# adaLN block with grouped-KV attention and a bilinear GLU: the q projections of later blocks as single whole-row products, a lead in smaller steps, and gate and up weights split by columns

## The chip, the cores and the metric

The kernel runs on one core of one Trainium2 chip. The metric is the device time of one execution in microseconds (us); for the kernel before, three executions were timed and the median counts. The engines are named as in the profile: PE does the matrix products (PEld is its weight load), DVE the reductions and elementwise work, ACT the activations, POOL (GpSimd) elementwise work in SBUF, SP issues DMAs. PE writes to PSUM, which has eight banks of 128 x 512 f32.

## The reference

One layer on x of 2048 x 512. A vector c gives six rows of modulation; the layer is attention and then a gated product, each behind a layer norm:

```python
mod = (_silu(c) @ w_mod).reshape(c.shape[0], 6, 1, -1)
h = _layernorm(x) * (1 + ca) + sa
q = (h @ wq)            # 32 heads of 16
k = h @ wk; v = h @ wv  # one head of 16, shared by all 32
p = _softmax(q @ k.T * 16 ** -0.5)
x = x + ga * ((p @ v) @ wo)
h = _layernorm(x) * (1 + cb) + sb
x = x + gb * (((h @ w_gate) * (h @ w_up)) @ w_down)   # width 1792
```

## The kernel before

**Numbers in halves.** f32 products take PE four passes, so the large ones are done on f16 pairs: a matrix is scaled, cut into a high and a low half, and a product is three terms (`TERMS`, line 413). `in_halves` (L374) makes the halves: ACT casts the high one, POOL scales the f32 tile in place and subtracts.

**Blocks, units, steps.** The 2048 queries are four blocks of 512 (`BT`); a block has eight units of four heads; a unit has 32 steps. In a step the main loop (L1104) issues two maximum products with their row maxima on DVE (`max_mm`, L516: the maximum of each row of scores, needed by the exponential), two score products with an exp on ACT each (`qk_exp`, L554), and at every odd step the product of the exps with v (`pv`, L563, four 32-column products in f32). The maxima run `LEAD` = 40 steps ahead of the rest, so they start in a *lead*: 40 steps with maxima alone, beside which the layer norm, k, v and q of the four blocks are prepared (`first`, L402, a table from step to work; `ln_tr` transposes, `k_mm` projects k, `h_halves` makes the f16 halves of the normed input, `v_mm` projects v in one go at step `V_STEP`). Before the lead stands a start, about 29 us, which loads, makes the first modulation and projects block 0's k and the first heads' q.

**q.** `q_proj` (L484) makes 128 columns of q for one block as a `Group` of twelve products. Two groups at a time run as a `duo` (L450): each product is cut into its upper and lower 64 rows, so that two 64-row products of the two groups run side by side; this holds two banks, misc and spare. Between its calls a duo yields, and `burst` (L1038) issues some of its pairs in a step. A group's evacuation is two ACT passes (L489, L490), one POOL subtraction and a DMA to DRAM, from where `load_q` (L503) later brings a unit's rows back. In the lead, `lead_fill` (L1068) bursts six pairs a step from step 18 on; what is left is queued for the main loop with a due step of 40 (`QDUE`). There `fill_gap` (L1013) is called at every even step, behind the second maximum product, and `pace` sets the rate by the due steps. The same queue later carries each block's output projection, second layer norm (`solo` items) and FFN groups.

**Banks.** Scores have two banks (tag sc) and, when no duo holds it, the bank spare as a third (`ps_sc`, L65); maxima have three, pv one, misc one.

**Side work.** A list of small steps (`late_weights`, L782) is issued from the main loop by `side_step` (L1054), one item at a time, each with a gap in steps to the next; an item with a PE product is only taken at odd steps, behind `pv`. In order: for each of the four late matrices (wo, wg, wu, wd) its slices are loaded and their squares added up on POOL (`square`), then the column sums are formed (`sums`, L829: four f32 products on 32 columns each, and a row maximum); the second modulation product (`m0`, four parts of four products, then `m1`, `m2`, `m3`); the scales; and then the split of wo, wg and wu into halves (`split`, L898: three POOL passes a slice, and one more for wo and wd, which are multiplied by the modulation rows gab and gbb). wg and wu are split in slices of 128 rows x 448 columns, all of wg first and then all of wu. wd follows in a list of its own.

**What the buffers share.** `kwb` holds the f32 tiles of the normed input (`hfs`, ten of them in turn) and, behind them, the sums of squares (`ssq`); wg and wu take the places of the two parts of w_mod.

Of the kernel before, what the change touches and what calls it, by code (L numbers as in the profile page):

```python
# [33 lines left out]
FILL0 = 18  # L34
QPRE = 20
QPRE0 = 26
# [4 lines left out]
NHF = 10  # L41
V_STEP = 34
DUE = 12
QDUE = 40
# [5 lines left out]
def adaln_mqa_glu_kernel(ctx: ExitStack, tc: tile.TileContext, x_in, wq_in, wk_in, wv_in, wo_in,  # L50
# [145 lines left out]
    ssq = kwb[:, 2 * NHF * BT:2 * NHF * BT + 2 * F].bitcast(F32)  # L196
# [7 lines left out]
    sck = consts.tile([128, 4], F32, name="sck")  # L204

    def ln_stats(i):
        if i % 2 == 0:
            stats[i // 2] = (work.tile([128, 4, 2], F32, name="st"), work.tile([128, 4], F32, name="ry0"),
                             work.tile([128, 4], F32, name="nb0"))
# [7 lines left out]
    def ln_norm(b):  # L217
        st, y, nb = stats[b]
        for i in range(2):
            xt = xts[2 * b + i]  # L220
            nc.vector.tensor_scalar(xt[:, 0, :], xt[:, 0, :], st[:, 2 * i, 0:1], y[:, 2 * i:2 * i + 1],
                                    op0=OP.subtract, op1=OP.mult)
            nc.scalar.activation(xt[:, 1, :], xt[:, 1, :], AF.Identity, bias=nb[:, 2 + i:3 + i],
                                 scale=y[:, 2 * i + 1:2 * i + 2])

    def ln_tr(b, ks=range(KC)):
        for k in ks:
            p = ps_sc()
            for t in range(4):
                nc.tensor.transpose(p[:, t * 128:(t + 1) * 128],  # L230
                                    xts[2 * b + t // 2][:, t % 2, k * 128:(k + 1) * 128], ident)
            nc.scalar.activation(hf(b, k), p, AF.Identity,
                                 bias=modT[0][:, k, 0:1], scale=modT[0][:, k, 32:33])
# [17 lines left out]
    def k_evac(b):  # L251
        cs = slice(b * BT, (b + 1) * BT)
        split_rows(kst[:, cs], pks[b], sck[:, 0:1], sck[:, 2:3], rows[:, 6:7])

    def ln_rstd(b):
        st, y, nb = stats[b]
        rstd_into(y, st[:, :, 1], 4)
        nc.gpsimd.tensor_tensor(nb[:, 0:2], st[:, 1:4:2, 0], y[:, 1:4:2], op=OP.mult)
        nc.gpsimd.tensor_scalar(nb[:, 2:4], nb[:, 0:2], -1.0, 0.0, op0=OP.mult, op1=OP.add)
# [68 lines left out]

    q0_mm(0)
# [6 lines left out]
    nc.gpsimd.tensor_scalar(inv[:, 0:1], kb[:, 4:5], 22.64 * 1.001 * 2.0 ** -15, 2.0 ** -45, op0=OP.mult, op1=OP.max)  # L336
# [31 lines left out]
    def wq_scales():  # L368
        nc.vector.reciprocal(fwd, inv)
# [4 lines left out]
    def in_halves(hi, lo, t, scale):  # L374

        nc.scalar.activation(hi, t, AF.Copy, scale=scale)
        nc.gpsimd.tensor_scalar(t, t, scale, 0.0, op0=OP.mult, op1=OP.add)
        nc.gpsimd.tensor_tensor(lo, t, hi, op=OP.subtract)  # L378

    def h_halves(b, ks=range(KC)):  # L380
        cs = slice(b * BT, (b + 1) * BT)
        for k in ks:
            in_halves(h16[:, 0, k, cs], h16[:, 1, k, cs], hf(b, k), fwd[:, 0:1])

    def wq_halves(ks):
        for k in ks:
            in_halves(wq[:, 0, k, :], wq[:, 1, k, :], wqst[k], fwd[:, 1:2])
# [7 lines left out]
    def last_rows():  # L395
# [6 lines left out]
    first = {0: lambda: (q0_mm(1, KA), wq_squares()), 1: lambda: (q0_mm(1, KB), wq_sum()),  # L402
             2: lambda: (q0_evac(1), ln_tr(1, KA), wq_scales()),
             3: lambda: (ln_tr(1, KB), ln_stats(6), h_halves(0, KA)), 4: lambda: k_mm(1, KA),
             5: lambda: (k_mm(1, KB), ln_stats(7), ln_rstd(3), h_halves(0, KB)),
             6: lambda: (k_evac(1), ln_norm(2)), 7: lambda: (ln_tr(2, KA), wq_halves(KA)),
             8: lambda: (ln_tr(2, KB), ln_norm(3), wq_halves(KB)), 9: lambda: k_mm(2, KA),
             10: lambda: (k_mm(2, KB), h_halves(1, KA)), 11: lambda: (k_evac(2), h_halves(1, KB)),
             12: lambda: ln_tr(3, KA), 13: lambda: ln_tr(3, KB), 14: lambda: (k_mm(3, KA), h_halves(2, KA)),
             15: lambda: (k_mm(3, KB), h_halves(2, KB)), 16: lambda: k_evac(3),  # L410
             17: lambda: (last_rows(), ev_scales()), 25: lambda: h_halves(3, KA), 27: lambda: (h_halves(3, KB), wv_halves())}
# [4 lines left out]
    def v_mm():  # L416
        p = vt["p"] = ps_pv()
        for k in range(KC):
            for i, (wl, hl) in enumerate(TERMS):
# [795 lines left out]
```

## Time and profile before

| | |
|---|---|
| median of three executions | 1780.48 us (1777.08 to 1782.25) |
| the profiled execution, its own time | 1779.66 us |
| its span in the profile | 1777.9 us |
| busy: PE, DVE, ACT, POOL | 1692.5, 1414.0, 1231.9, 509.8 us |
| first exp of unit 0 | at 105.07 us |
| mean granted clock of TensorE | 0.993 |

The page gives busy times and shares, a chain of waits that ended last, and groups of instructions by line. A group's row is: line, engine, operation, output and inputs, shapes and count, then its busy time and the mean length of one in ns, then the idle time of the engine before them and what ended it. A row of the timeline is: start and length in us, engine, line, operation, names, shapes and count (several that follow closely are merged), and in brackets the idle time before and its releaser. A row of the windows is: the stretch and its length, for each engine its busy time and number of instructions, then the granted clock, the share of the DMA engines and GB/s. The ends of matrix products are modelled and overlap, so distances between their starts tell more than their lengths.

### The profile page before, as it was taken

The numbers are of one execution on the slowest core, as the hardware profiler recorded it, in microseconds if no ns is written. First come the engines' busy times: TensorE is split into PE (matmuls) and PEld (weight loads), VectorE is DVE, ScalarE is ACT, GpSimd is POOL, SyncE is SP. The second block draws the span as 40 slices with busy tenths as digits, with TensorE's granted clock in tenths as the row PEclk, the third lists the DMA queues.
The fourth block names the chain that finished last, engine by engine and source line by source line (L and its number), as shares of the span: only waits on it lengthen the run. The fifth ranks groups of instructions, "written<-read, shape, count | busy, mean of one in ns | idle before, by whom it ended". The sixth has DMA issues, their size and how long they took to land.

```text
span 1777.9 us, 32413 instructions
## 1 busy us (share of the span) xinstructions
PE 1692.5 (95%) x12727; PEld 558.3 (31%) x12727; DVE 1414.0 (80%) x2348; ACT 1231.9 (69%) x2301; POOL 509.8 (29%) x706
## 2 busy tenths in 40 slices
PE   6899999989989999999999999999999999999999
PEld 2432222222222333333323333333323333324444
DVE  7777999989987888888898888888898899920310
ACT  4567888878876777777777777777787777774210
POOL 5833453618555941110022111010022011100330
PEclk9899999999999999999999999999999999999999
DMA  5222221212221200000100000000100000001000
GB/s 194 88 77 78 64 81 50 68 45 66 78 63 38 74 20 13 9 16 20 40 21 16 9 5 20 3 14 21 39 21 16 9 16 9 11 4 41 19 0 24
DMA packets 49797, 66.60 MB, mean 37 GB/s; under 512 B 16166, under 2 KB 30314, under 8 KB 49644
## 3 DMA queue, kind: packets, MB, share of 16 engines
q1 hardware_dynamic: 48060, 64.33, 11.6%
q8 instruction: 100, 1.64, 0.4%
q14 instruction: 53, 0.43, 0.1%
q10 hardware_dynamic: 1584, 0.20, 0.1%
HBM read 51.12 MB, written 8.92 MB: 34 GB/s over the span
## 4 chain that ended last, share of the span: by engine, by line
PE 80%; ACT 9%; DVE 5%; POOL 3%; DMA 1%; issue 1%; SPq 0%; POOLq 0%; ACTq 0%
PE pv L568 26%; PE misc L448 19%; PE mx L521 13%; PE sc L559 12%; PE misc L479 7%; ACT P L561 6%; DVE mpart L523 4%; ACT ev L574 1%; DMA wmA<-in_w_mod_dram 1%; POOL h L378 1%; POOL wu L918 0%; PE mxt L535 0%; DVE x L650 0%; ACT qf L490 0%; ACT q L489 0%
## 5 line engine op out<-in xcount | busy, mean ns | idle before, releaser
L523 DVE TENSOR_REDUCE mpart<-mx 128x1 f32<-128x512 f32 x2048 | 1298.1, 683 | 154.6 <-PE sc L559 122.9
L561 ACT ACTIVATE P<-sc 128x512 f32<-128x512 f32 x2048 | 1096.8, 597 | 326.0 <-PE sc L559 322.5
L559 PE MATMUL sc<-sst,kst 50*128 50x512 f16 x2048 | 631.1, 380 | 40.9 <-ACT P L561 35.7
L521 PE MATMUL mx<-kst,sst 48*128 48x512 f16 x2048 | 648.4, 382 | 19.3 <-DVE mpart L523 15.6
L568 PE MATMUL pv<-P,vst 128*32 128x512 f32 x4096 | 547.8, 607 | 0.0
L521 PEld LDWEIGHTS <-sst 48*128 48x128 f16 x2048 | 161.2, 94 | 586.4 <-issue 520.0
L448 PE MATMUL misc<-h2T,wu 64*128 64x512 f16 x1008 | 254.9, 376 | 2.9 <-POOL wu L917 2.1
L448 PE MATMUL misc<-h2T,wg 64*128 64x512 f16 x1008 | 254.7, 376 | 0.0
L742 POOL TENSOR_SCALAR glu<-gf 128x512 f16<-128x512 f32 x56 | 34.7, 621 | 543.5 <-DVE gf L741 543.5
L559 PEld LDWEIGHTS <-kst 50*128 50x128 f16 x2048 | 138.1, 94 | 100.7 <-issue 59.2
L568 PEld LDWEIGHTS pv<-P,vst 128*32 128x32 f32 x4096 | 80.9, 108 | 167.1 <-issue 163.9
L448 PEld LDWEIGHTS <-wu 64*128 64x128 f16 x1008 | 94.9, 94 | 63.2 <-POOL wu L917 2.6
L448 PEld LDWEIGHTS <-wg 64*128 64x128 f16 x1008 | 94.5, 94 | 52.9 <-issue 2.2
L741 DVE TENSOR_TENSOR gf<-misc,g 128x512 f32<-128x512 f32 x56 | 38.3, 683 | 89.6 <-PE misc L479 62.9
L448 PE MATMUL misc<-wd,glu 64*128 64x512 f16 x840 | 105.7, 375 | 0.0
L601 POOL TENSOR_TENSOR oc<-oc,rr 128x512 f32<-128x512 f32 x15 | 19.1, 1274 | 267.2 <-DMA rr<-ri 194.5
L735 ACT ACTIVATE g<-misc 128x512 f32<-128x512 f32 x56 | 33.5, 598 | 69.1 <-PE misc L479 63.4
L743 POOL TENSOR_TENSOR glu<-gf,glu 128x512 f16<-128x512 f32 x56 | 64.8, 1157 | 4.7
L448 PEld LDWEIGHTS <-glu 64*128 64x128 f16 x840 | 43.7, 94 | 45.6 <-issue 1.7
L825 POOL TENSOR_TENSOR wsl<-wsl 128x448 f32<-128x448 f32 (+1 forms) x40 | 39.1, 977 | 57.0 <-DMA wsl<-in_B_w_up_dram 31.1
L448 PE MATMUL misc<-h,wq 64*128 64x512 f16 x384 | 53.0, 391 | 2.4 <-ACT qf L490 2.4
L479 PE MATMUL misc<-wd,glu 128*128 128x512 f16 x252 | 55.1, 379 | 0.0
(218 smaller groups left out, 913.9 us busy)
## 6 DMA issues: line engine op xcount, KB each, us to landing
wsl<-in_B_w_gate_dram SPq DMA_DIRECT2D x32, 224.0 KB
wsl<-in_B_w_up_dram SPq DMA_DIRECT2D x32, 224.0 KB
wsl<-in_B_w_down_dram SPq DMA_DIRECT2D x28, 256.0 KB
sst<-qd SPq DMA_DIRECT2D x186, 32.0 KB
qd<-q SPq DMA_DIRECT2D x16, 256.0 KB
oc<-ev SPq DMA_DIRECT2D x128, 32.0 KB
rr<-ri SPq DMA_DIRECT2D x16, 256.0 KB
xl<-in_A_x_dram SPq DMA_DIRECT2D x16, 256.0 KB
```

The lines of the kernel that those rows point to most:

```text
L448: nc.tensor.matmul(p, left[64 * r:64 * r + 64], right[64 * r:64 * r + 64], start=start, stop=stop)
L479: nc.tensor.matmul(p, left, right, start=i == 0, stop=i == g.n - 1)
L521: nc.tensor.matmul(m, s[64 * a:64 * a + 48, p, t * 128:(t + 1) * 128], kst[64 * a:64 * a + 48, kc * 512:(kc + 1) * 512], start=True, stop= ...
L523: nc.vector.tensor_reduce(mparts[u][:, a, p, t, kc:kc + 1], m, axis=AX.X, op=OP.max)
L559: nc.tensor.matmul(t, kst[64 * a:64 * a + 50, kt * 128:(kt + 1) * 128], s[64 * a:64 * a + 50, p, :], start=True, stop=True)
L561: nc.scalar.activation(ptl[u, kt, p][:, a, :], t, AF.Exp)
L568: nc.tensor.matmul(pvb[u][32 * j:32 * j + 32, :], vst[:, kt, :], ptl[u, kt, p][:, a, :], start=(kt == 0), stop=(kt == KT - 1))
L735: nc.scalar.activation(st["g", f], p, AF.Copy, scale=2.0 ** -45)
L741: nc.vector.tensor_tensor(gf, p, st["g", f], op=OP.mult)
L742: nc.gpsimd.tensor_scalar(st["glu"][:, 0, f, :], gf, 1.0, 0.0, op0=OP.mult, op1=OP.add)
L743: nc.gpsimd.tensor_tensor(st["glu"][:, 1, f, :], gf, st["glu"][:, 0, f, :], op=OP.subtract)
L825: nc.gpsimd.tensor_tensor(acc if i == 0 else t, t, t, op=OP.mult)
```

## The change

- **q.** In the lead only two duos remain (block 0), in bursts given by a table (`Q_BURSTS`: 4 + 2 + 2 + 2 + 2, 6 + 6, 4 + 4 + 4, 4 + 4 + 4). The twelve groups of blocks 1 to 3 are queued for the main loop one by one as kind "one": `plain` products over all 128 rows on the bank misc alone, two a burst (`MOST_ONE`), the next group three steps after the last at the earliest (`ONE_WAIT`), due at step 236. Scores keep the bank spare meanwhile. The second half of a group's evacuation (`rest`) is put off to the start of the next step.
- **The lead.** `first` is rewritten: k of blocks 2 and 3 and the transposes of block 3 come in quarters, v in quarters over four steps, the squares of wq later. Ahead of it, the scale of h's halves is made early and put into the affine step of the layer norm for blocks 1 to 3 (`hsb`, with `sckb` to undo it in k), which saves POOL a pass; for blocks 0 and 1 the high half is cast by POOL instead of ACT. There are 14 buffers instead of 10 for the normed tiles, and the sums of squares share their place. The rows for q of unit 1 are loaded at step 29 instead of 26.
- **Modulation.** The second modulation product moves from the side list to steps 25 to 31 of the lead, on a score bank.
- **Side work.** Each column sum is done in four items of a quarter of the columns each; wg and wu are split in the order of the columns, wg's and wu's four row slices of one column range before the next range; gab and gbb are scaled once, so wo and wd need one POOL pass less a slice.

```diff
-FILL0 = 18
-QPRE0 = 26
+QPRE0 = 29
+MOST_ONE = 2
+ONE_WAIT = 3
-NHF = 10
-V_STEP = 34
+NHF = 14
+V_STEP = 33
+M_STEP = 25
+Q_BURSTS = {16: 4, 17: 2, 18: 2, 19: 2, 20: 2, 22: 6, 23: 6, 30: 4, 31: 4, 32: 4, 37: 4, 38: 4, 39: 4}
-QDUE = 40
+QDUE = 236
...
+    nc.gpsimd.tensor_scalar(inv[:, 0:1], kb[:, 4:5], 22.64 * 1.001 * 2.0 ** -15, 2.0 ** -45, op0=OP.mult, op1=OP.max)
+    nc.vector.reciprocal(fwd[:, 0:1], inv[:, 0:1])
+    nc.vector.tensor_scalar(hsb, modT[0][:, :, 0:64:32], fwd[:, 0:1], None, op0=OP.mult)
+    nc.gpsimd.tensor_scalar(sckb, sck, inv[:, 0:1], 0.0, op0=OP.mult, op1=OP.add)
     q0_mm(0)
...
+    def in_halves(hi, lo, t, scale, first):
+        if first is nc.scalar:
+            nc.scalar.activation(hi, t, AF.Copy, scale=1.0 if scale is None else scale)
+        if scale is not None:
+            nc.gpsimd.tensor_scalar(t, t, scale, 0.0, op0=OP.mult, op1=OP.add)
+        if first is not nc.scalar:
+            nc.gpsimd.tensor_scalar(hi, t, 1.0, 0.0, op0=OP.mult, op1=OP.add)
         nc.gpsimd.tensor_tensor(lo, t, hi, op=OP.subtract)
...
-            in_halves(h16[:, 0, k, cs], h16[:, 1, k, cs], hf(b, k), fwd[:, 0:1])
+            in_halves(h16[:, 0, k, cs], h16[:, 1, k, cs], hf(b, k),
+                      None if b else fwd[:, 0:1], nc.scalar if b > 1 else nc.gpsimd)
...
+    first = {0: lambda: q0_mm(1, KA), 1: lambda: (q0_mm(1, KB), ln_stats(6)),
+             2: lambda: (q0_evac(1), ln_tr(1, KA)), 3: lambda: (ln_tr(1, KB), ln_norm(2), h_halves(0, KA)),
+             4: lambda: (k_mm(1, KA), ln_stats(7), ln_rstd(3)), 5: lambda: (k_mm(1, KB), h_halves(0, KB)),
+             6: lambda: (k_evac(1), wq_squares()), 7: lambda: ln_tr(2, KA),
+             8: lambda: (ln_tr(2, KB), last_rows(), wq_sum()), 9: lambda: (k_mm(2, (0,)), ln_norm(3), wq_scales()),
+             10: lambda: (k_mm(2, (1,)), wq_halves(KA)), 11: lambda: k_mm(2, (2,)),
+             12: lambda: (k_mm(2, (3,)), wq_halves(KB)), 13: lambda: (k_evac(2), ln_tr(3, (0,))),
+             14: lambda: (ln_tr(3, (1,)), h_halves(1, KA)), 15: lambda: ln_tr(3, (2,)),
+             16: lambda: (ln_tr(3, (3,)), h_halves(1, KB)), 17: lambda: k_mm(3, (0,)), 18: lambda: k_mm(3, (1,)),
+             19: lambda: k_mm(3, (2,)), 20: lambda: k_mm(3, (3,)), 21: lambda: (k_evac(3), h_halves(2, KA)),
+             22: lambda: h_halves(2, KB), 24: lambda: (ev_scales(), wv_halves()), 26: lambda: h_halves(3, KA),
+             28: lambda: h_halves(3, KB)}
...
             nc.scalar.activation(q16[:, 0, :], p, AF.Copy, scale=qvs[:, 0:1])
+            def rest():
+                nc.scalar.activation(qf, p, AF.Copy, scale=qvs[:, 0:1])
+                nc.gpsimd.tensor_tensor(q16[:, 1, :], qf, q16[:, 0, :], op=OP.subtract)
+                d = dram.tile([128, 2, BT], F16, name=f"qd{b}_{ch}")
+                nc.sync.dma_start(d, q16)
+                qd[b, ch] = d
+            after(1, rest)
...
-            items.append((2,) + sums(m))
-        items += [(2, m0(k), m1 if k == KC - 1 else None) for k in range(KC)] + [(2, m2, None), (4, nothing, m3)]
+            items += [(2,) + sums(m, j) for j in range(4)]
...
-        items += pipelined(list(range(n2)))
-        return items, pipelined(list(range(n2, len(sl))))
+        by_column = sorted(range(KC, n2), key=lambda n: sl[n][1][1].start)
+        items += pipelined(list(range(KC)) + by_column)
+        return items, pipelined(list(range(n2, len(sl)))), [m0(k) for k in range(KC)] + [m1, m2, m3]
...
+            if kind == "one":
+                cur.update(gen=plain(what), left=what.n, turn=what.n, second=True, due=due, swapped=-9, one=True)
+            else:
+                begin(step, what, due)
+        if cur["one"]:
+            burst(step, max(1, min(int(credit[0]), cur["left"], MOST_ONE)))
+            return
...
+        if n in Q_BURSTS:
+            if cur["gen"] is None:
+                begin(n, qtwos.popleft(), QDUE)
+            burst(n, Q_BURSTS[n])
+        m, v = n - M_STEP, n - V_STEP
+        if 0 <= m < len(mod_rows):
+            mod_rows[m]()
+        if 0 <= v < KC:
+            v_mm(v)
...
     for two in qtwos:
-        fill.append(([0, 0], "duo", two, QDUE))
+        fill.extend(([0, 0], "one", one, QDUE) for one in two)
```

More of the change, by code (lines that the diff above doesn't have):

```diff
@@ L252, in k_evac @@
         cs = slice(b * BT, (b + 1) * BT)
-        split_rows(kst[:, cs], pks[b], sck[:, 0:1], sck[:, 2:3], rows[:, 6:7])
+        sc = sckb if b else sck
+        split_rows(kst[:, cs], pks[b], sc[:, 0:1], sc[:, 2:3], rows[:, 6:7])
     def ln_rstd(b):
@@ L827, in square, with sums @@
                 nc.gpsimd.tensor_tensor(acc, acc, t, op=OP.add)
-        def sums(m):
+        def sums(m, j):
+            w = (D if m > 1 else GC) // 4
             def f():
@@ L901, in load @@
             def load():
-                if m == 0 and "g" not in W:
+                if m < 2 and "g" not in W:
                     W["g"] = big.tile([128, 2, KC, F], F16, name="wg", tag="wg")
@@ L988, in adaln_mqa_glu_kernel @@
     fill = deque()
-    cur = {"gen": None, "left": 0, "swapped": -9}
+    cur = {"gen": None, "left": 0, "swapped": -9, "wait": 0, "one": False}
     credit = [0.0]
@@ L997, in pace @@
         for _, kind, what, due in fill:
-            n += 4.0 if kind == "solo" else 2 * what[0].n
+            n += 4.0 if kind == "solo" else what.n if kind == "one" else 2 * what[0].n
             kept = RESERVE / PAIR if due > (NB * UB - 1) * NSTEP else 0.0
@@ L1003, in open_gate @@
     def open_gate(step):
-        if not fill:
+        if not fill or (fill[0][1] == "one" and step < cur["wait"]):
             return False
@@ L1035, in begin @@
     def begin(step, two, due, tags=("misc", "spare")):
-        cur.update(gen=duo(*two, tags=tags), left=2 * two[0].n, turn=two[0].n, second=False, due=due, swapped=-9)
+        cur.update(gen=duo(*two, tags=tags), left=2 * two[0].n, turn=two[0].n, second=False, due=due, swapped=-9,
+                   one=False)
     def burst(step, n):
@@ L1044, in burst @@
             if swap is None:
-                cur["gen"], cur["left"] = None, 0
+                cur["gen"], cur["left"], cur["wait"] = None, 0, step + ONE_WAIT
                 return
@@ L1111, in adaln_mqa_glu_kernel @@
             drain_posts()
-            spare["scores"] = not spare["held"] and cur["gen"] is None and not (fill and fill[0][1] == "duo" and open_gate(step))
+            spare["scores"] = not spare["held"] and (cur["gen"] is None or cur["one"]) and not (fill and fill[0][1] == "duo" and open_gate(step))
             max_half(0)
@@ L1127, in adaln_mqa_glu_kernel @@
                 credit[0] = min(credit[0] + pace(step), 9.0)
-                if credit[0] >= 1.0:
+                one = cur["one"] if cur["gen"] else fill[0][1] == "one"
+                if credit[0] >= (MOST_ONE if one else 1.0):
                     fill_gap(step)
```

108 lines of the change are left out of this document (43 added, 65 removed).

## Prediction

> **What bounds the kernel now.** I read the page first (span, chain), then the windows cut at the starts of the units, then the timeline of single cycles, then the groups by line.
>
> ```profile
> span 1777.9 us, 32413 instructions
> ...
> PE 80%; ACT 9%; DVE 5%; POOL 3%; DMA 1%; issue 1%; SPq 0%; POOLq 0%; ACTq 0%
> ```
>
> The chain that ended last is 80% PE, but that is a mean over stages. The windows part them: two for the lead (from the first reduce to the first exp), then units 0, 1, 3, 9 and 10 of the main loop, each cut where the first exp of a unit starts.
>
> ```profile
> core 0: us, PE busy (x) PEld busy (x) DVE busy (x) ACT busy (x) POOL busy (x), PEclk, DMA share, GB/s
> 29.31:66.54 37.23, 31.53 (x118) 13.41 (x119) 30.45 (x54) 25.56 (x42) 27.69 (x39) 0.94 0.22 85
> 66.54:105.07 38.53, 34.28 (x290) 15.36 (x290) 28.69 (x49) 13.57 (x23) 22.58 (x28) 0.93 0.13 47
> 105.07:157.58 52.51, 49.93 (x399) 16.45 (x398) 41.24 (x67) 40.57 (x77) 16.94 (x16) 1.00 0.22 73
> 157.58:203.76 46.18, 42.55 (x299) 10.99 (x297) 40.16 (x66) 36.68 (x70) 21.81 (x22) 0.96 0.27 83
> 245.26:285.52 40.26, 36.54 (x259) 9.01 (x257) 39.85 (x67) 33.89 (x68) 22.53 (x23) 1.00 0.21 63
> ...
> 499.90:559.40 59.50, 50.97 (x360) 14.89 (x358) 43.91 (x75) 40.21 (x75) 36.06 (x67) 0.91 0.17 49
> 559.40:608.10 48.70, 48.59 (x405) 16.10 (x406) 43.09 (x71) 37.00 (x70) 38.51 (x43) 1.00 0.22 63
> ```
>
> Three regimes. A unit without filling work (unit 3, 40.26 us) has DVE busy 39.85: the row maxima bound it. From unit 10 on, the projections of earlier blocks fill PE: 48.59 busy of 48.70, and the change touches nothing that costs time there. Between lie the places that it edits: the lead (75.76 us with DVE busy 59.14, so 16.6 idle), units 0 and 1 (q of later blocks: 18.17 us over two units of 40.26), unit 5 (the second modulation product), and unit 9, which takes 59.50 where its neighbour with more products takes 48.70.
>
> A unit is 16 cycles of two steps. One from unit 3:
>
> ```profile
> 256.39 0.60 PE L559 MATMUL sc<-sst,kst 50*128 50x512 f16 x2
> 256.62 0.63 PE L521 MATMUL mx<-kst,sst 48*128 48x512 f16 x2
> 256.84 2.07 ACT L561 ACTIVATE P<-sc 128x512 f32<-128x512 f32 x4 [0.40 <-PE sc L559]
> 256.88 0.39 PE L559 MATMUL sc<-sst,kst 50*128 50x512 f16 x1
> ...
> 257.49 0.37 PE L559 MATMUL sc<-sst,kst 50*128 50x512 f16 x1 [0.22 <-ACT P L561]
> ...
> 257.86 1.07 PE L568 MATMUL pv<-P,vst 128*32 128x512 f32 x8
> ...
> 258.86 0.39 PE L521 MATMUL mx<-kst,sst 48*128 48x512 f16 x1
> ```
>
> The cycle from 256.39 to 258.86 is 2.47 us. DVE reduces almost without a pause (39.85 of 40.26); ACT rests 0.40. PE has its hole in one place: between the pair at 256.88, which needs about 0.23 (the step from 256.39 to 256.62), and the score product at 257.49 that waits for a bank, so about 0.38. The new q products go into the queue just ahead of 256.88, at the even step, and so use exactly that hole. What follows 257.49 (last maximum, pv, next pair) has no slack: DVE waits for what comes behind pv.
>
> **Part by part: q of later blocks.** Six double groups become 12 single ones of 12 whole-row products on the bank of misc, two a burst: 72 bursts, spread to step 236. Before, four doubles ran in units 0 and 1 and four in the lead; now two run in the lead. No whole-row f16 product occurs in a cycle of before; the nearest rows are the four 128-row transposes put at the same place in unit 9, and the tail's whole-row products:
>
> ```profile
> 531.06 0.39 PE L521 MATMUL mx<-kst,sst 48*128 48x512 f16 x1
> ...
> 531.29 0.38 PE L521 MATMUL mx<-kst,sst 48*128 48x512 f16 x1
> ...
> 531.60 0.66 PE L693 MATMUL misc<-ident,n 128*128 128x128 f32 x4
> ...
> 532.19 0.39 PE L521 MATMUL mx<-kst,sst 48*128 48x512 f16 x1
> ...
> 533.73 0.39 PE L521 MATMUL mx<-kst,sst 48*128 48x512 f16 x1
> 534.15 0.69 DVE L523 TENSOR_REDUCE mpart<-mx 128x1 f32<-128x512 f32 x1 [0.18 <-PE sc L559]
> ```
>
> ```profile
> L479 PE MATMUL misc<-wd,glu 128*128 128x512 f16 x252 | 55.1, 379 | 0.0
> ```
>
> From the pair at 531.29 to the next at 532.19 are 0.90 us, 0.67 more than the 0.23 of neighbours; the cycle (531.06 to 533.73) becomes 2.67, PE never waits and DVE idles 0.18. So without the transposes PE alone needs 2.00. Two products of 55.1/252 = 0.219 are 0.44; going from 48-row to 128-row work costs 0.31 instead of 0.23 (531.29 to 531.60), and I take the same 0.08 back, together 0.60. PE then needs 2.60 in a cycle that takes 2.47: **0.13 a burst, 9.4 us for 72**. The bounds are 0 (the hole is wider than it looks) and 0.20 (the transposes' whole cycle, with an evacuation of its own in it).
>
> The row of 0.31 is where the Trainium skill speaks against this change: its page "TensorEngine Tiling (Array Packing)", section "Key Properties", says that a switch of the tiling mode, not merely of the tile, drains TensorE. The double form stays in 64-row mode, next to 48-row work; the single form leaves and returns in each of 72 bursts. The trace agrees that a switch costs, and puts 0.08 us on it; were it nothing, the burst would be 0.44, the cycle 2.44, and the sum 9.4 us lower.
>
> Each of the 12 groups is evacuated by two ACT passes, now a step boundary apart but with no exp between them (the later half runs first in the next step):
>
> ```profile
> L489 ACT ACTIVATE q<-misc,qvs 128x512 f16<-128x512 f32 x16 | 11.1, 694 | 19.4 <-PE mx L521 11.5 <-PE misc L448 4.4 <-POOL kwb L377 1.4
> ...
> 173.98 0.91 PE L559 MATMUL sc<-sst,kst 50*128 50x512 f16 x2 [1.05 <-ACT P L561]
> ...
> 174.86 1.93 PE L568 MATMUL pv<-P,vst 128*32 128x512 f32 x8
> ```
>
> Two passes of 0.69 (the second has the same shape) are 1.39 us in a cycle where ACT rests 0.40: up to 0.99 late, and behind ACT the exps, then the score banks, PE's queue and DVE wait. Three score banks absorb a part; I take 0.75, between 0.3 and 1.4. Twelve are **9.0 us**. New q: 18.4. It replaces the excess of units 0 and 1, 18.17, of which about 1.1 is the sum of squares of wo that stays: 17.1. **Net +1.3 us**, with ends -11 and +13. So the single form wins little by itself; its use is that two doubles leave the lead.
>
> **The lead.** Idle of DVE by its largest pieces:
>
> ```profile
> L523 DVE TENSOR_REDUCE mpart<-mx 128x1 f32<-128x512 f32 x80 | 50.6, 682 | 14.6 <-PE mx L521 14.5
> ...
> 63.53 1.29 DVE L523 TENSOR_REDUCE mpart<-mx 128x1 f32<-128x512 f32 x2 [1.76 <-PE mx L521]
> 69.75 1.29 DVE L523 TENSOR_REDUCE mpart<-mx 128x1 f32<-128x512 f32 x2 [1.28 <-PE mx L521]
> 72.60 1.89 DVE L523 TENSOR_REDUCE mpart<-mx 128x1 f32<-128x512 f32 x3 [1.57 <-PE mx L521]
> 83.63 1.29 DVE L523 TENSOR_REDUCE mpart<-mx 128x1 f32<-128x512 f32 x2 [0.23 <-PE mx L521]
> 93.61 1.29 DVE L523 TENSOR_REDUCE mpart<-mx 128x1 f32<-128x512 f32 x2 [1.65 <-PE mx L521]
> 97.93 1.29 DVE L523 TENSOR_REDUCE mpart<-mx 128x1 f32<-128x512 f32 x2 [1.34 <-PE mx L521]
> ```
>
> The three of 62 to 73 us (4.6) are the last k projection, held up by the halving of h on POOL and ACT, and then the first double at a lowered clock. With 14 instead of 10 buffers for h, one POOL pass less a tile (blocks 1 to 3), ACT freed of two blocks' casts and k in quarters, I let 4.0 go. V in one block cost 1.65 and 1.34; in four pieces 2.5 of that go. Each burst of six cost 0.23; two doubles fewer are eight bursts, 1.8. Against that come the four quarters of the modulation product, each in a step where DVE needs 1.2 us and PE little else (0.4 in all), and k quarters that share steps 17 to 20 with q bursts (1.2). **Net -6.7**, ends 0 and -14.6 (all of the idle). One wait may be new: q of unit 1 is loaded at step 29 instead of 26, three steps ahead of its first use; 0 to 2 us, I take 0 within the net. Four small operations ahead of the lead sit in DVE's and POOL's queues before the evacuation of k and q: **+0.3**, ends 0 and 1.
>
> **The modulation product** leaves unit 5. There each quarter stood behind pv, the place without slack:
>
> ```profile
> 358.90 0.60 PE L790 MATMUL misc<-wmB,silr 128*32 128x512 f32 x2
> ...
> 359.87 0.39 PE L521 MATMUL mx<-kst,sst 48*128 48x512 f16 x1
> ...
> 220.97 0.62 DVE L839 TENSOR_REDUCE cmx<-mx 128x1 f32<-128x448 f32 x1 [0.52 <-PE mx L836]
> ```
>
> 0.97 from its first product to the next pair, 0.09 of it the change of mode: 0.88 four times, and about 0.6 for the row's copy and transposes: **-4.1**. The sums of squares in quarters cost the same PE and DVE time (four times 0.52 + 0.62 before, sixteen times about 0.3 after): **0**, ends -3 and +3. They push the list of side work ten steps back.
>
> **wg and wu by columns.** The first pair of FFN groups read wu before POOL had split its last rows of wu:
>
> ```profile
> 546.29 0.39 PE L448 MATMUL misc<-h2T,wu 64*128 64x512 f16 x1 [2.14 <-POOL wu L917]
> 548.50 1.51 DVE L523 TENSOR_REDUCE mpart<-mx 128x1 f32<-128x512 f32 x2 [4.12 <-PE mx L521]
> 549.22 1.94 PE L568 MATMUL pv<-P,vst 128*32 128x512 f32 x8
> ```
>
> DVE lost 4.12; the lowered clock behind it cost another 0.87 on pv (1.94 for 1.07) and about 1.0 on the pairs beside it. Counted by the gaps in the list (an item of 2.5 comes every third step), the split begins ten steps later than before, at step 27 of unit 6; the four slices of wo and the eight of the first 448 columns of wg and wu are done 13 items on, at step 2 of unit 8, a unit and a half before their use, and the next 448 within unit 8: **-6.0**. The end of the split, step 10 of unit 10, lies before those columns are used, at three double groups a unit. POOL is as loaded as before while the normalisation of block 0 waits on it in unit 9; that rest of unit 9 I leave. Scaling gab and gbb once saves POOL passes nobody waits for: 0.
>
> **Sum:** -6.7 + 0.3 + 1.3 - 4.1 + 0 - 6.0 = -15.2. Profiled execution 1779.66 us (span 1777.9), 0.05% under the median 1780.48: 1764.5 by its time, and I state 1764.
>
> **Rivals.**
> - *The bursts are hidden.* For it: PE's hole of 0.38 and ACT's rest. Against: PE's 2.67 cycle. 9.4 less: 1755. Chance 0.20.
> - *Slower: the burst is serial.* If DVE follows every delay at that place, as it followed the modulation product, a burst adds its whole 0.60: 43.2 instead of 9.4, +33.8, 1798. It decides from 0.13 + 15.2/72 = 0.34 a burst on (no gain), 0.42 for a loss of 0.3%. Against: the transposes at that very place cost 0.20. Chance 0.08.
> - *The clock falls after evacuations.* At 174.86, after two evacuations, pv took 1.93 instead of 1.07; with pairs about 1.5 us each time, 12 times 18: 1782, no change. Against: groups now end singly. Chance 0.10; half as often gives 1773. The Trainium skill, "TensorE: Matmul & The Clock Gate", Part 1, lets the clock halve after an idle window of some 3.4 us, by which no evacuation would do it; the trace shows it halved after a longest PE wait of 1.05 (at 173.98).
> - *The lead keeps its length*, since what leaves PE returns as modulation, as ACT's order or as the late load of q: 1771. Chance 0.10.
>
> My forecast, 1758 to 1770: 0.52. **Chances.** About 0.3%, 5.3 us, is what a measurement can tell. Faster by more: forecast, hidden bursts, lead, and a part of the clock's case, 0.83; within, 0.08; slower 0.09. The range 1750 to 1776 leaves out the serial burst, the full clock case and a little below.
>
> **What would show it.** Lead near 69 us to the first exp; units 0 to 7 near 42.5 each with cycles of 2.6 where L479 appears and 2.47 elsewhere; unit 5 without L790; no POOL wait of a wu product in unit 9, which falls to about 53; units from 10 on unchanged. Wrong if units 2 to 7 exceed 44, if the lead stays above 74, or if another wait fills unit 9.

## The result and the profile after

The changed kernel takes **1756.82 us** (median of four, 1754.42 to 1757.59) beside 1780.28 before (now the median of four executions as well): a ratio of 0.9868, 95% interval 0.985 to 0.9885, or 23.5 us. The forecast was 1764, range 1750 to 1776. The profiled execution took 1754.42 us, 25.2 less than the profiled one of before; the spans differ as much (1752.6 beside 1777.9). First the page:

```profile
span 1752.6 us, 32268 instructions
...
PE 1687.6 (96%) x12679; PEld 541.3 (31%) x12679; DVE 1413.7 (81%) x2363; ACT 1228.3 (70%) x2293; POOL 494.2 (28%) x687
...
PE 82%; ACT 9%; DVE 4%; POOL 2%; issue 1%; DMA 1%; SPq 0%; ACTq 0%; POOLq 0%
...
L548 DVE TENSOR_REDUCE mpart<-mx 128x1 f32<-128x512 f32 x2048 | 1297.9, 684 | 131.5 <-PE sc L584 112.0
```

DVE has the same work (1413.7 us for 1414.0), PE has 5 us less and POOL, which is busy for 28% only, 16 less: the gain is in the main waiting that went. As before, the page says only that. The place is in the windows, cut at the first exp of a unit: the lead, units 0, 1, 4, 5, 9 and 10.

```profile
core 0: us, PE busy (x) PEld busy (x) DVE busy (x) ACT busy (x) POOL busy (x), PEclk, DMA share, GB/s
29.25:95.24 65.99, 61.03 (x350) 22.17 (x351) 59.00 (x104) 30.06 (x52) 41.01 (x58) 0.97 0.19 68
95.24:138.51 43.27, 38.53 (x280) 9.87 (x280) 40.10 (x70) 34.54 (x68) 12.01 (x11) 0.96 0.17 53
138.51:180.35 41.84, 40.07 (x279) 8.49 (x276) 40.13 (x67) 35.80 (x68) 17.40 (x18) 1.00 0.25 76
266.37:309.44 43.07, 41.57 (x313) 9.75 (x311) 41.22 (x72) 36.84 (x71) 17.07 (x17) 1.00 0.22 63
309.44:351.92 42.48, 41.22 (x285) 8.84 (x284) 40.15 (x67) 36.85 (x70) 27.72 (x25) 1.00 0.27 83
483.24:534.89 51.65, 47.12 (x365) 14.77 (x362) 43.95 (x74) 40.35 (x75) 38.76 (x67) 0.97 0.23 66
534.89:583.84 48.95, 48.84 (x409) 16.16 (x407) 43.09 (x71) 37.00 (x69) 31.58 (x36) 1.00 0.21 61
```

The lead has the same DVE work (59.00 us for 59.15) in 9.8 us less; unit 9 is near its PE-bound neighbour. Cut at the first exp of each unit in both (the prediction's own windows, but for that of unit 0, began 1.5 to 3 us early), before and after compare so:

| us | before | after | difference |
|---|---|---|---|
| lead, first maximum to first exp | 75.76 | 65.99 | -9.8 |
| units 0 and 1 | 100.19 | 85.11 | -15.1 |
| units 2 to 7 | 251.91 | 257.53 | +5.6 |
| unit 9 | 59.90 | 51.66 | -8.2 |
| units 8 and 10 to 31 | 1108.69 | 1108.74 | 0.0 |
| tail behind the last exp | 152.12 | 154.36 | +2.2 |

Each column is one profiled execution, and some rows differ between executions of the same code. The old lead, unaltered in the kernel with the columns alone (below), took 72.86; the new one 64.38 in most profiles of the kernels below; unit 9 with the new order and three buffers took 51.7 to 54.4 in nine profiles.

q has been spread: units 2 to 7 pay for what units 0 and 1 save. Here is one cycle with a burst, PE's rows of the timeline:

```profile
281.96 0.39 PE L546 MATMUL mx<-kst,sst 48*128 48x512 f16 x1
...
282.19 0.38 PE L546 MATMUL mx<-kst,sst 48*128 48x512 f16 x1
282.50 0.60 PE L500 MATMUL misc<-h,wq 128*128 128x512 f16 x2
283.04 0.39 PE L546 MATMUL mx<-kst,sst 48*128 48x512 f16 x1
...
283.58 1.06 PE L593 MATMUL pv<-P,vst 128*32 128x512 f32 x8
284.57 0.39 PE L546 MATMUL mx<-kst,sst 48*128 48x512 f16 x1
```

From pair to pair 281.96 to 284.57 is 2.61 us (2.62 in the mean of the cycles with a burst and nothing else). PE has no gap. The burst starts 0.31 behind the maximum product of 48 rows, where neighbours of 48 rows stand 0.23 apart, and the next pair follows 0.54 behind the burst's start, where two products of 0.22 need 0.44: 0.08 more on the way in and 0.10 on the way out. And this is ACT at an evacuation:

```profile
271.66 1.08 ACT L586 ACTIVATE P<-sc 128x512 f32<-128x512 f32 x2 [0.37 <-PE sc L584]
272.63 0.69 ACT L510 ACTIVATE q<-misc,qvs 128x512 f16<-128x512 f32 x1
273.20 0.70 ACT L513 ACTIVATE qf<-misc,qvs 128x512 f32<-128x512 f32 x1
273.77 3.06 ACT L586 ACTIVATE P<-sc 128x512 f32<-128x512 f32 x6
```

From 271.66 to 276.8 ACT has no pause: eight exps and two passes, one behind the other. The two cycles take 5.53 us instead of the 5.09 that one with a burst and one without would, so an evacuation costs 0.44.

### The profile page after: what moved, and what is told of

The parts are those of the page before. It is cut to its first block, busy times and chain, and to the rows that moved or that the text cites. A ratio compares the mean times of both kernels' runs of the same rounds, so it can differ in the third digit from the quotient of the medians.

```text
span 1752.6 us, 32268 instructions
## 1 busy us (share of the span) xinstructions
PE 1687.6 (96%) x12679; PEld 541.3 (31%) x12679; DVE 1413.7 (81%) x2363; ACT 1228.3 (70%) x2293; POOL 494.2 (28%) x687
## 4 chain that ended last, share of the span: by engine, by line
PE 82%; ACT 9%; DVE 4%; POOL 2%; issue 1%; DMA 1%; SPq 0%; ACTq 0%; POOLq 0%
PE pv L593 27%; PE misc L469 18%; PE mx L546 14%; PE sc L584 12%; PE misc L500 9%; ACT P L586 6%; DVE mpart L548 3%; ACT ev L599 1%; DMA wmA<-in_w_mod_dram 1%; ACT q L510 1%; ACT qf L513 0%; PE misc L252 0%; DVE x L675 0%; PE mxt L560 0%; DMA wsl<-in_B_w_gate_dram 0%
## 5 line engine op out<-in xcount | busy, mean ns | idle before, releaser
L546 PEld LDWEIGHTS <-sst 48*128 48x128 f16 x2048 | 155.6, 93 | 575.4 <-issue 517.4
L853 POOL TENSOR_TENSOR kwb<-kwb,wsl 128x448 f32<-128x448 f32 (+1 forms) x40 | 47.7, 1191 | 3.1
L183 POOL TENSOR_SCALAR rv<-st 128x1 f32<-128x1 f32 (+1 forms) x20 | 4.5, 227 | 149.7 <-DVE st L686 133.8
```

The lines of the kernel that those rows point to most:

```text
L546: nc.tensor.matmul(m, s[64 * a:64 * a + 48, p, t * 128:(t + 1) * 128], kst[64 * a:64 * a + 48, kc * 512:(kc + 1) * 512], start=True, stop= ...
L853: nc.gpsimd.tensor_tensor(acc, acc, t, op=OP.add)
```

## Experiments

**The price of a burst.** The first two vary the number of products in it. The first lets a burst start at a credit of one:

```diff
-                if credit[0] >= (MOST_ONE if one else 1.0):
+                if credit[0] >= 1.0:
```

> The changed kernel, but a burst of the single q groups starts at a credit of 1 instead of 2, so that most bursts hold one product and some two. In the changed kernel's trace a cycle with a burst of two takes 2.62 us and one without 2.47. Theory (the burst only costs what it exceeds PE's hole: PE needs 2.00 + 0.16 for the two changes of mode + 0.22 for each product): a cycle with one product needs 2.38, so stays at 2.47; some 68 singles and 38 doubles cost 5.5 instead of 10.4 us, 1752. Rival (each change of mode is a fixed price whatever the burst holds): 106 bursts at 0.15 are 16, 5 more than now, 1762.

Measured: 1755.17 us, ratio 0.9865 (0.9849 to 0.988), so the 1752 of the theory was not reached. Thirteen cycles hold a single product and nothing else; they take 2.48 in the mean:

```profile
330.02 0.39 PE L546 MATMUL mx<-kst,sst 48*128 48x512 f16 x1
...
330.56 0.39 PE L500 MATMUL misc<-h,wq 128*128 128x512 f16 x1
...
332.49 0.39 PE L546 MATMUL mx<-kst,sst 48*128 48x512 f16 x1
```

2.47 from pair to pair: a single product is free. Most bursts stayed at two (58 cycles, and 28 with one product, for 38 and 68 expected), since the credit grows during the pauses between groups, so units 0 to 7 gained 1.2 us only. The other way, three at a time:

```diff
-MOST_ONE = 2
+MOST_ONE = 3
```

> The changed kernel with three products a burst (48 bursts instead of 72). Theory (PE's hole): a cycle with a burst needs 2.00 + 0.16 + 0.66 = 2.82, 0.35 over 2.47; 48 of them are 16.8 instead of 10.4 us, so 6 slower than the changed kernel: 1763. Rival (a fixed price for each change of mode): 48 at 0.15 are 7, 3 faster: 1753.

Measured: 1759.27, ratio 0.9883 (0.9865 to 0.99); units 0 to 7 take 348.11 for 342.64, 5.5 more, of which 0.8 lies in the third cycle of unit 0 (3.26 for 2.47), where the clock was still at 0.50, for 6.83 us in all.

```profile
284.56 0.39 PE L546 MATMUL mx<-kst,sst 48*128 48x512 f16 x1
...
285.10 0.82 PE L500 MATMUL misc<-h,wq 128*128 128x512 f16 x3
...
287.39 0.39 PE L546 MATMUL mx<-kst,sst 48*128 48x512 f16 x1
```

2.83 us. With one, two and three products a cycle takes 2.47, 2.62 and 2.83. PE's own sum, 2.00 + 0.16 + 0.22 for each product, gives 2.38, 2.60 and 2.82, and below DVE's 2.47 it does not show: the three cases lie within 0.02 of that line, and the rival, the same price for each burst whatever it holds, falls. The 0.16 (the way from 48-row to 128-row products and back, 0.08 and 0.10 in the rows above) is part of it: without it two products would need 2.44 and be hidden, which they were not. The Trainium skill, "TensorEngine Tiling (Array Packing)", section "Key Properties", says that changing the mode drains TensorE; the trace agrees that the change costs, 0.08 and 0.10 us here, but no run here shows that a drain is what takes them.

**The evacuation.** The second pass another step later:

```diff
-            after(1, rest)
+            after(2, rest)
```

> The changed kernel, but the second ACT pass of a q group's evacuation comes two steps after the first instead of one, so that exps stand between the two. An evacuation costs 0.44 us in the changed kernel's trace (2.11 + 0.95 + 0.95 + 1.52 against a cycle of 2.62 and one of 2.47). Theory (1.39 us of ACT in one piece outrun ACT's rest of 0.40 a cycle, and the three score banks do not hold all of it): in two pieces of 0.69, each in a cycle of its own or nearly so, it falls to about 0.2: 12 groups, 3 us faster, 1754. Rival (the cost is the delayed bank of misc or the POOL pass, not ACT's order): no change, 1757.

Measured: 1757.91, ratio 0.9879 (0.9864 to 0.9894). The steps around an evacuation are 1.52, 1.52, 0.95 and 1.52, together 5.51 for 5.53. My theory of the piece that fits or doesn't falls: ACT's total over the two cycles fits as the bound (two cycles of exps, 4.14, and 1.39 of passes are 5.53), wherever the passes stand within them. The edit has a price of its own in the lead, and its profile shows where. There too the second pass comes a step later, and with it the write of q to DRAM, so the maxima of unit 1 wait for their rows, and steps 31 and 32 of the lead take 4.8 us for 2.7:

```profile
85.01 0.37 PE L546 MATMUL mx<-kst,sst 48*128 48x512 f16 x1 [0.88 <-DMA sst<-qd]
```

So the late load of q for unit 1 costs nothing in the changed kernel, and 2.1 us when the rows come one step later.

**Double or single.** The same q work in the loop, but as six duos with both passes together, due early enough for the bank:

```diff
-QDUE = 236
+QDUE = 60
...
-            after(1, rest)
+            rest()
...
-        fill.extend(([0, 0], "one", one, QDUE) for one in two)
+        fill.append(([0, 0], "duo", two, QDUE))
```

> The changed kernel, but the twelve q groups of the main loop run as six double groups of 64-row products at the pace of the kernel before (due at step 60, both ACT passes together): the lead of the change with the q of before. Theory (a double costs about 4.3 us of the loop, as four did in units 0 and 1 before; two single groups cost 12 times 0.15 and 2 times 0.44, 2.6): six doubles 26 instead of 16, 10 us slower than the changed kernel, 1767. Rival (only what leaves the lead counts, the form does not): within 3 us of 1757.

Measured: 1770.9, ratio 0.9949 (0.9934 to 0.9965). Units 0 to 7 take 360.51, 17.9 more than after; the cycles show why: 2.91 with eight 64-row products, 3.27 with twelve, 4.37 with a pair of evacuations. 2.8 of it lies in the first two cycles, 6.51 and 3.59 for 3.05 and 4.27, where the lead's last duo is evacuated. So once this much q is in the loop, the duos cost 14 us of time (10 were expected), and the rival falls. The run changes three things together, the form, the second pass and the pace (step 60 for 236); what each is worth wasn't taken apart.

**The columns alone**, on the kernel before:

```diff
-        items += pipelined(list(range(n2)))
+        by_column = sorted(range(KC, n2), key=lambda n: sl[n][1][1].start)
+        items += pipelined(list(range(KC)) + by_column)
```

> The kernel before with one part of the change alone: wg and wu split by columns in turn. Theory (unit 9 waited for the last row slices of wu): unit 9 falls from 59.9 to about 52, all other units stay to a tenth, 8 us faster than before: 1772. Rival (unit 9 is long because POOL is busy with the split at all, and fell because the list moved): the wait for wu goes but comes back as waits of the normalisation, 3 us or less: 1777.

Measured: 1773.21, ratio 0.9964 (0.9951 to 0.9977). Unit 9 goes from 59.90 to 53.31 us (-6.6), about as the theory had it. Part of this is the clock: in unit 9 of before it was at 0.50 for 10.2 us in all, here for 3.4. The reverse, the new order of work with the old split, wasn't tried.

**What is left in unit 9.** It took 51.65 beside 48.95 for unit 10. In the profile after, POOL's rows there are:

```profile
496.81 0.64 POOL L946 TENSOR_SCALAR wsl<-wsl,sca 128x448 f32<-128x448 f32 x1 [2.77 <-DMA wsl<-in_B_w_gate_dram]
497.54 0.56 POOL L947 TENSOR_SCALAR wg<-wsl 128x448 f16<-128x448 f32 x1
498.18 1.04 POOL L948 TENSOR_TENSOR wg<-wsl,wg 128x448 f16<-128x448 f32 x1
499.30 0.22 POOL L183 TENSOR_SCALAR rv<-st 128x1 f32<-128x1 f32 x1
```

and behind them ACT's normalisation, which holds up the exps:

```profile
501.84 0.81 ACT L693 ACTIVATE n<-x,nb,ry 128x512 f32<-128x512 f32 x1 [2.29 <-POOL nb L689]
```

I read this as POOL's split standing in the way, and paused the list around the normalisation:

```diff
-        if side and step >= side_next[0] and (step % 2 or side[0][1] is nothing):
+        if side and not 8 * NSTEP + 29 <= step < 9 * NSTEP + 14 and step >= side_next[0] and (step % 2 or side[0][1] is nothing):
```

> The changed kernel, with the list of side work paused from step 29 of unit 8 to step 14 of unit 9, while block 0 is normalised. Theory (what is left of unit 9's excess, steps of 3.1 and 4.1 us, is POOL holding the chain of the reciprocal roots behind the split, and behind a slice that has not landed): unit 9 falls from 52 to about 48.5, 3.5 us faster, 1753; the columns of the split come 17 steps later, still ahead of their use. Rival (the chain itself, eight small POOL operations a tile, is what ACT waits for): less than 1 us, and the delayed split gives a wait in units 10 to 12.

Measured: 1752.94, ratio 0.9851 (0.9827 to 0.9875), but unit 9 takes 52.61, within the 51.7 to 54.4 of the nine profiles with three buffers and no pause: the theory fails. The profiled execution is 2.1 us shorter than the one of after by its lead and its tail (64.38 and 153.54); why the median is 3.9 lower, its one profile does not show. What its unit 9 waits for is another load:

```profile
488.67 0.75 DVE L675 SCALAR_TENSOR_TENSOR x<-misc,sca,xl 128x512 f32<-128x512 f32 x1 [0.24 <-PE misc L469]
...
489.44 0.33 SPq L652 DMA_DIRECT2D xl<-in_A_x_dram  x1
...
492.31 0.75 DVE L675 SCALAR_TENSOR_TENSOR x<-misc,sca,xl 128x512 f32<-128x512 f32 x1 [2.30 <-DMA xl<-in_A_x_dram]
```

The load of x's last tile is issued the moment the sum before it has read its own x (488.67 + 0.75 is 489.42): it waited for a buffer. Slices and x share one tag with three buffers, and slices that had been loaded just ahead of the pause, at 470.83 and 474.10, held two of them. So the second wait and the 2.77 us of POOL may be one thing, a lack of buffers. Five instead of three, wherever the tag is named (one line of five), and nothing else:

```diff
-        xl = work.tile([128, D], F32, name="xl", tag="xl", bufs=3)
+        xl = work.tile([128, D], F32, name="xl", tag="xl", bufs=5)
```

> The tag xl, which the loads of x for the residual sum share with the side list's weight slices, gets five buffers instead of three; nothing else changes. Theory: in unit 9 of the changed kernel the wait is one for buffers: the split of a slice on POOL waits for a load that could only be issued once a buffer came free (L946 waited 2.77 us for its DMA at 496.81), and the inverse standard deviation of the normalisation stands behind that split on POOL. With two more buffers the loads are issued earlier, POOL is done with its slices earlier and steps (9,7) and (9,9), 3.13 and 4.10 us, lose 2 to 4 us together: unit 9 at 48 to 50 instead of 51.66, the time 1753 to 1755. Rival: POOL's own work on the slice (0.64 + 0.56 + 1.04 us) is in the way, whenever its load lands, and unit 9 stays within 0.7 of 51.66.

Measured: 1753.16, ratio 0.9853 (0.9838 to 0.9867), as the theory had it. Unit 9 is at its neighbour's length, 3.0 to 5.7 us below the profiles with three buffers, and its clock is at 1.00:

```profile
483.57:532.25 48.68, 46.52 (x365) 14.45 (x363) 43.63 (x74) 40.46 (x76) 38.87 (x67) 1.00 0.21 60
```

Its POOL rows:

```profile
491.70 0.64 POOL L946 TENSOR_SCALAR wsl<-wsl,sca 128x448 f32<-128x448 f32 x1
...
493.08 1.03 POOL L948 TENSOR_TENSOR wg<-wsl,wg 128x448 f16<-128x448 f32 x1
495.81 0.23 POOL L183 TENSOR_SCALAR rv<-st 128x1 f32<-128x1 f32 x1 [1.70 <-DVE st L686]
```

There POOL does the same slices without a wait for a load, is done at 494.11 and then waits for DVE. It was the landing of the slices, not the work on them. The 3.4 us at half clock that unit 9 had in after are gone as well and are part of the gain.

With pause, buffers and smaller bursts together:

> Three edits on the changed kernel: the side list pauses from step 29 of unit 8 to step 14 of unit 9, the tag xl has five buffers, and a burst starts at a credit of one. With the pause alone, unit 9 kept 52.61 us: there x of the last tile was loaded only when the sum of the tile before had released its buffer, at 489.44, and landed at 492.31 (DVE waited 2.30 us), since two slices that were loaded ahead of the pause held two of three buffers. Theory: pause and buffers together take both waits away; steps (9,6), (9,7) and (9,9) fall to about 1.7 each from 3.92, 3.59 and 2.33, and unit 9 to 46.5 to 48.5; the time is 1749 to 1752 beside 1756.8 of the changed kernel. Rival: the normalisation's own chain over DVE, POOL and ACT is the wait, whatever is in front of it: unit 9 stays above 50.5 and the time above 1752.

Measured: **1751.85**, ratio 0.9844 (0.983 to 0.9859), the lowest median here. Unit 9 is 48.68 again: with the buffers the pause adds nothing. It is 28.4 us under its own runs of before (1780.23).

**The lead.** Three edits each undo one part. V in one block at step 34:

```diff
-        if 0 <= v < KC:
-            v_mm(v)
-            if v == KC - 1:
-                posts.append(v_evac)
+        if v == 1:
+            for k in range(KC):
+                v_mm(k)
+            posts.append(v_evac)
```

> The changed kernel with v in one block of 48 products at step 34 of the lead instead of four of 12. Theory (what PE does in one go beyond three banks of maxima, DVE waits out: the block cost 1.65 and 1.34 us before): the lead becomes about 2 us longer. Rival (the lead was slow there because of its two last double groups, and the block hides as well): within 0.5 us.

Measured: 1757.95, ratio 0.9879 (0.9854 to 0.9903). DVE's row behind the block:

```profile
88.34 1.89 DVE L548 TENSOR_REDUCE mpart<-mx 128x1 f32<-128x512 f32 x3 [2.10 <-PE mx L546]
```

Steps 33 to 36 take 1.20, 3.57, 1.21 and 1.20 instead of 1.35, 1.47, 1.36 and 1.21: 1.8 us for the quarters, as expected. Then ten buffers for the tiles of h:

```diff
-NHF = 14
+NHF = 10
```

> The changed kernel with 10 instead of 14 buffers for the tiles of h in the lead; nothing else. Theory (the prediction's: the buffers are one of the causes of the shorter lead): tiles of block 2 and 3 wait again for the halving of blocks 0 and 1 on POOL, around steps 8 and 13 to 16 of the lead; the lead grows by 2 to 5 us from the 64.4 that most runs of the new order take, and the time by the same, to 1759 to 1762. Rival: with smaller steps and POOL's shorter halving the tiles come free in time; the lead stays within 0.7 us of 64.4 and the time at 1755 to 1757.5.

Measured: 1756.09, ratio 0.9869 (0.9853 to 0.9886); the lead is 64.39 us, the same step for step as in most profiles of the new order. Theory wrong, rival right: the four buffers bring nothing that a profile shows. Last, the casts of blocks 0 and 1 on ACT again:

```diff
-                      None if b else fwd[:, 0:1], nc.scalar if b > 1 else nc.gpsimd)
+                      None if b else fwd[:, 0:1], nc.scalar)
```

> The changed kernel with the first cast of every tile of h on ACT again (in the changed kernel POOL does it for blocks 0 and 1); POOL keeps its other passes and the steps stay where the change put them. Theory (the prediction's: ACT, freed of two blocks' casts, is one of the causes of the shorter lead): eight casts of about 0.7 us come back into ACT's queue at steps 3, 5, 14 and 16, ahead of evacuations for which PE and DVE wait; the lead grows by 1 to 4 us from the 64.38 that the undisturbed profiles of the new order show, most of it at steps 3 to 9. Rival: it is the order of the steps alone (sums of squares of wq later, the normalisation split over both engines); then steps 0 to 8 stay within 0.5 us of their 17.8 and the lead within 0.7 of 64.38, the time between 1755 and 1757.5.

Measured: 1761.51, ratio 0.99 (0.9873 to 0.9926). The lead as a window of this kernel:

```profile
28.62:97.22 68.60, 63.08 (x350) 23.44 (x351) 58.83 (x104) 34.45 (x60) 36.27 (x51) 0.93 0.18 65
```

and of the kernel with bursts of one or two, whose lead is that of the new order as it stands:

```profile
28.84:93.22 64.38, 59.43 (x350) 21.85 (x351) 58.97 (x104) 30.06 (x52) 41.17 (x59) 1.00 0.19 69
```

4.2 us more, with a clock of 0.93 for 1.00. The size is just above the 1 to 4 expected, the place is another: steps 0 to 8 keep their 17.8 us, and the growth is at steps 9 to 16. Step 9 grows by 1.15 at full clock: DVE waits 1.88 for POOL there, 0.40 in the kernel with bursts of one or two. The other 3.0 lie in steps 11 to 16, in a stretch at half clock:

```profile
50.77 0.17 DVE L382 RECIPROCAL fwd<-inv 128x2 f32<-128x2 f32 x1 [1.88 <-POOL inv L379]
52.92:63.16 10.24, 10.24 (x37) 4.35 (x38) 7.40 (x12) 5.83 (x9) 8.54 (x9) 0.50 0.20 82
```

(the first is a row of the timeline, the second of the windows). How much of the 3.0 the casts cause isn't shown, since the clock also falls there without them. Steps 11 and 12 took 1.32 and 1.38 in eight profiles with the casts on POOL, but 2.4 and 1.9 in two (after among them) with 3.41 us at 0.50, and 2.58 and 2.55 in the kernel with the second pass later, with 6.83. That the casts cost something stands: all four executions (1759.73 to 1763.79) are longer than those of after, with medians 4.7 apart where the medians of before differ by 1.4.

In the kernel with the columns alone, whose lead is the old one, steps 0 to 8 took 21.2: those 3.4 us come neither from the casts nor from the buffers, so from the rest of what changed there, the order of the steps above all, which I did not take apart further.

**The tail** is 2.2 us longer after. The first row in which it differs is the read of the row sums:

```profile
1606.01 1.41 DVE L782 SCALAR_TENSOR_TENSOR x<-misc,sca,x 128x512 f32<-128x512 f32 x2 [34.38 <-PE misc L469]
1611.42 0.35 DVE L617 RECIPROCAL rc<-rc 128x32 f32<-128x32 f32 x1 [4.00 <-DMA rc<-rs]
```

and in before:

```profile
1633.49 1.41 DVE L756 SCALAR_TENSOR_TENSOR x<-misc,sca,x 128x512 f32<-128x512 f32 x2 [34.38 <-PE misc L448]
1637.21 0.35 DVE L592 RECIPROCAL rc<-rc 128x32 f32<-128x32 f32 x1 [2.31 <-DMA rc<-rs]
```

The same small read, issued right behind the same two writes of the output, is awaited 1.7 us less there. The tiles in DRAM come in another order after the change, so I put them into the order of before:

```diff
-                d = dram.tile([128, 2, BT], F16, name=f"qd{b}_{ch}")
+                d = dt["q", b, ch]
```

(likewise the row sums, their inverses and the modulation row, all made ahead in before's order).

> The changed kernel with its tiles in DRAM (q, the sums of the exps, their reciprocals, the modulation rows) given places in the order in which the kernel before made them; nothing else differs. The part behind the last exp took 152.1 us before and 152.0 in the kernel with columns alone, but 154.4 to 155.4 in the changed kernel and the three made from it, from the load of the sums for the last reciprocal on, which takes 3.9 us from issue to the next issue instead of 2.2. Theory (the place of a small tile in DRAM decides, since the issues stand at the same times): the part returns to 152, 2.5 us faster, 1754. Rival (it hangs on which DMA rings or engines the packets meet, by the count of transfers before, or on something else): it stays at 154 to 155, 1757.

Measured: 1756.3, ratio 0.987 (0.984 to 0.9899), tail 153.66. The theory falls: from the issue of the read to its use are 3.38 us here, 3.54 in after, 3.44 to 3.57 in the other kernels with q in single groups, and 1.82 to 1.85 in the three with duos in the loop (before, the columns alone, the duos of above, whose tails are 152.12, 152.00 and 152.07). The long read goes with the single groups, not with the place in DRAM; by what way, a thousand microseconds later, stays open. The tails also differ by the clock: 3.41 us at 0.50, from a time between 1614 and 1626 us on, stand in the profiles with tails of 155.1 to 155.5 and in none of those with 153.5 to 154.4.

## Why the prediction was right, step by step

The sign and the range were right, and 1764 was 7 us too high. Its terms against the two profiled executions (q, modulation and the list are parted from one another by comparison with the kernel with duos in the loop):

| term, us | predicted | measured |
|---|---|---|
| lead and start | -6.4 | -9.8 |
| q of later blocks, net | +1.3 | about -3.3 |
| modulation product | -4.1 | about -4.0 |
| sums of squares, rest of the list | 0 | -2.2, by difference |
| wg and wu by columns, unit 9 | -6.0 | -8.2 (alone -6.6) |
| tail | not in the sum | +2.2 |
| sum | -15.2 | -25.3 |

**q.** The mechanism held and the burst was sized well: 2.62 a cycle for 2.60 forecast, from a transpose in unit 9 and a product of the tail. The evacuation was taken at 0.75 and is 0.44: I reckoned ACT's lateness within one cycle, where its rests of two cycles pay for it.

In the cycle of an evacuation the burst costs nothing more, since ACT bounds it: 3.07 with two products, and 3.07 with one in the kernel with bursts of one or two. Nor does it in a cycle that the unit's transposes make longer anyway: 2.82 and 2.63 with a burst, 2.85 and 2.63 without. So the twelve groups cost about 12.9 us for 18.4 forecast: 11.3 in units 2 to 7, which take 257.5 with them and 246.2 without (247.3 in the kernel with duos in the loop, which has no q left there, less 1.0 in which a sum waits for POOL), and 1.6 in unit 1. What they replace is about 18.6, not 17.1, since the prediction's windows of units 0 and 1 ended 1.5 us early.

Against that stands a step that I had at nothing, the start of the loop, where the last duo of the lead is evacuated. PE's rows and then DVE's, and the windows before and at that place:

```profile
99.00 1.07 PE L584 MATMUL sc<-sst,kst 50*128 50x512 f16 x2 [0.48 <-ACT P L586]
...
100.02 1.93 PE L593 MATMUL pv<-P,vst 128*32 128x512 f32 x8
```

```profile
102.53 3.16 DVE L548 TENSOR_REDUCE mpart<-mx 128x1 f32<-128x512 f32 x5 [1.70 <-PE sc L584]
```

```profile
95.88:99.29 3.41, 2.22 (x9) 0.50 (x9) 2.62 (x5) 3.41 (x7) 1.46 (x2) 1.00 0.48 154
99.29:102.70 3.41, 3.29 (x15) 0.59 (x15) 1.24 (x3) 1.45 (x4) 1.44 (x2) 0.50 0.55 194
```

pv takes 1.93 for 1.06: the granted clock is 0.50 for 3.41 us. In the 3.41 us before, PE was busy for 2.22, and its longest wait was 0.96 (at 95.89). 2.4 us once; the rival that had this at every evacuation is refuted, for the other twelve left pv at 1.06. The Trainium skill, "TensorE: Matmul & The Clock Gate", Part 1, has the clock halve after an idle window of about 3.4 us; here it fell after waits of 0.5 to 1 us in a row, and the measurement decides.

The rival "bursts are hidden" came nearest to the time with its 1755, by accident: a burst of two is not hidden, one of one would be.

**The lead** is the term that was mis-sized: -9.8 for the -6.4 of lead and start (the start kept its time, 29.25 for 29.31). Luck is in the -9.8. The new lead, profiled at 65.99, usually takes 64.38, but the old one took 75.76 in the profile of before and 72.86 in the kernel with the columns alone, so the gain lies between 6.9 and 11.4. Of the 2.9 between the two profiles of the old lead, 2.8 stand at steps 18 and 19, where before was at half clock for 6.83 us from 65.44 on; the prediction names this lowered clock, but gives it no term.

Among the causes, 4.0 went to four together: buffers, one POOL pass less, casts and k in quarters. The buffers are worth nothing, the casts 1.2 or more (4.2 with the clock), and the POOL pass and k in quarters weren't tried apart from the order of the steps, which the sum did not hold apart at all. Between the old lead of the columns alone and the usual new one there are 3.4 us in steps 0 to 8, 2.1 in steps 9 to 16 and 3.9 behind them; but work moved between these stretches (k of block 3 from steps 14 and 15 to 17 to 20), so they are no prices. V in pieces is worth 1.8 (2.5 let go). One of the two waits that the prediction gave to V was not V's: the 1.65 at 93.61 ends before V's first product,

```profile
94.80 2.77 PE L421 MATMUL pv<-h,wv 128*32 128x512 f16 x48
```

and stands behind a duo's products. The duos that left the lead (1.8 let go) weren't tried apart either.

**Sums in quarters.** Taken as the same work, 0, with an end of -3. A whole sum made its cycle 3.28 us in the mean of three, and in two of them the next one 2.79; a quarter makes 2.68, and beside an evacuation it disappears. So a sum costs 0.84 in four quarters alone, for 0.9 to 1.2 whole: at most 1.4 of the 2.2 for four sums. The rest of the list was not taken apart.

**Modulation** was sized right (unit 5 takes 45.20 with it and a whole sum, 40.24 with neither in the kernel with duos in the loop), and moved without a price that I can see: steps 25 to 31 of the lead take 1.18 to 1.45.

**Unit 9.** The columns alone gave 6.6 for 6.0, and the mechanism held: no product waits for wu in unit 9 after, and the first columns of the split are done at step 1 of unit 8 (step 2 forecast), the last at step 11 of unit 10 (step 10 forecast). That a rest of unit 9 would stay was right, but the reason, POOL's load of work, was not: it was three buffers.

**What would show it:** lead near 69 (66.0, usually 64.4); units 0 to 7 near 42.5 (42.8 in the mean), cycles 2.6 and 2.47 (yes); unit 5 without the modulation product (42.48 for 45.20); unit 9 near 53 (51.7, its lowest; up to 54.4 in the profiles of other kernels with its code); units from 10 on unchanged (1063.4 and 1063.3). Of its signs of being wrong one came: unit 6, with 44.66, exceeds the mark of 44. It holds the last sum and the scales of the list beside q, and takes 43.16 without q.

## What to carry to other kernels

Price filling work by the engine that bounds the cycle it falls into: a product of 0.22 us was free up to the bound, cost its full length beyond it, and nothing at all where another engine was already the bound. When an engine waits for a load, look up when the load was issued: where it started the moment a buffer came free, more buffers were the mend, and moving the work was not. Before a part of one profile is given to an edit, look at the same part in profiles of kernels that share its code: the lead here differed by 1.6 us and unit 9 by 2.7 with nothing changed in them.

## What was not expected of the hardware

The granted clock is 1.00 or 0.50 in these traces, and within the span each stretch at 0.50 lasts 3.41 us or two, three or four times that. It need not follow the code alone: ahead of steps 11 and 12 of the new lead PE was busy for 2.1 of 3.41 us in four profiles looked at, and in three of these the clock then fell, in the fourth it did not. With the casts on ACT, where PE was busy for 1.35 of the 3.41 us before, it stayed down for 10.24 us. And one read of 16 KB behind two writes of 256 KB had two lengths, about 1.8 us with duos in the loop and about 3.5 without; its cause is open.
